# Expert 0's token list summed on chip instead of read back from DRAM

## The chip, the cores and the metric

The kernel runs on one core of a Trainium2 chip. Its engines are named as the profile names them: PE (TensorE), DVE (VectorE), ACT (ScalarE), POOL (GpSimd) and SP (SyncE, which only issues DMAs here). The metric is the device time of one execution in microseconds; the median of three runs is given.

## The reference

Eight heads of memory attention per batch give x, and x goes through a mixture of eight experts in which each row takes the two with the largest noisy logits:

```python
a = softmax(phi, axis=2)                          # 8 batches, 8 heads, 576 rows, 32 memories
k_m, v_m = a^T k, a^T v                           # per batch and head
x = softmax(q k_m^T / 8) v_m                      # 4608 rows of 512
noisy = x @ w_gate + log1p(exp(x @ w_noise)) * noise
top2, top2_w = two largest of 8, softmaxed
for e in range(8):                                # 512 -> 1024 -> 512, all fp32
    out[rows of e] += top2_w * (relu(x[rows of e] @ w1[e]) @ w2[e])
```

## The kernel before, in words

**Attention.** Batches go in four pairs P = 0 to 3. Each batch has two load units (kv, q, phi; u = 0 to 15); each pair has five groups of rows (n = 0 to 19, up to 256 rows each) for which `c_s`, `c_soft1`, `c_soft2`, `c_tr` and `c_av` make scores, softmax, transposition and product. `c_soft2` multiplies by the reciprocal sum on POOL for n < GN and on DVE otherwise. `c_av` also makes the gate logits `lg` and writes the rows to `xs` in DRAM.

**Routing.** `gate(P, j0, j1)` runs once per pair for P = 0, 1, 2 (nine blocks of 128 rows) and in two parts for the last pair. It takes the logits to the two chosen experts (DVE, ending in the mask `gmb`), counts positions within each expert's list with products against a triangle of ones (PE, lines 665 to 670), and turns them to slots: `gidx`, or `pidx` in the last pair (line 692). For P = 0, 1, 2 an entry per row and choice (row id, gate weight) is written by 18 indirect DMAs from POOL into the lists `lst` in DRAM (line 709), from entry tiles `gent0` and `gent1` in turn. `lists` reads them back on SP (line 840) into `ltall` (128 slots x tile x expert).

**Last pair.** Its entries never go through DRAM before they are needed: `onehots` and `onehot_gates` build one-hot matrices of slot and tile on DVE in fp32, PE sums them to 128 x 80 ids and gates, and `merge` adds them into `ltall` after converting the read ids (the CAST of line 590).

**Experts.** Each expert has up to ten tiles of 128 rows. Expert 0's tiles 0 to 5 form the groups g0, g1, g2 of two tiles, which run as early fill for PE among the attention: `gather` fetches the rows with indirect DMAs (line 884), splits them to two f16 halves on ACT and DVE (`ghalf`), and transposes them with a DMA (line 899); `mm1` makes 96 products of 256 columns per group (line 1062), `mm2` 48 of 512 (line 1092). `NEED` says which pair's routing each of g0, g1, g2 needs: (1, 1, 2). Group g3 (tiles 6 to 9, 448 rows) and experts 1 to 7 (products and sums of halves, lines 937 to 1122) follow the last routing. The transposed early rows lie in `stg0`, `stg1`, `stg2`, which expert 1's weight loads also use.

**Order.** A planner gives each step a time from tables of numbers (`PRI`, `ADJ`, `BUF`) and a list scheduler turns the times into one order per engine. `BUF` m0, m1, m2 are the attention groups before which g0, g1, g2 may split their rows.

Of the kernel before, what the change touches and what calls it, by code (L numbers as in the profile page):

```python
# [38 lines left out]
BUF = dict(kvs=3,  phs=3,  qs=2,  et=2,  es=3,  pe=4,  at=3,  xr=4,  st0=1,  st1=1,  ptr=3,  px=2,  mps=3,  xa=3,
           w1=8,  w2=11,  zg=11,  ws=1,  m0=4,  m1=18,  m2=26,  r0=11,  r1=1,  zr=6,  GN=6,  na=1,  nb=22)  # L40
ADJ = dict(s2=(-0.305, -0.749, 0.433, -2.721, 0.107, -0.302, -4.821, -1.222, 0.27, 1.101, 0.051, -0.491, -2.472,
           -2.668, -1.78, -0.576, -2.138, -1.591, -0.804, -1.961),  z=(0.057, -0.272, -1.907, -1.817, -1.721,
           -1.848, -0.055, 0.645, 0, -0.029, -0.085, 1.721, 1.537, 1.865, 1.687, 1.656, 1.687, 2.746, 3.506, 3.003,
           3.003, 1.944, 1.944, 2.087, 1.944, 2.06, 1.944, 1.857, 1.395, 1.512, 1.485, 1.253, 0.1, 1.799, 1.389,
           2.141, 2.115, 3.031),  avb=(0, -1.482, -1.014, -1.627, -1.533, -0.831, -4.141, -3.022, -1.439, -0.672,
           -0.029, -1.474, -2.98, -2.403, -2.514, -2.116, -1.783, -6.14, -2.999, -3.138),  av=(0.104, 0.01, 0.092,
           0.139, 0, 0.031, 0.031, 0.07, -0.107, 0.02, 0, -0.387, -0.146, 0.26, -0.531, 0.259, -0.092, -0.315,
           -0.755, -1.542),  q=(-0.032, 0.356, -0.035, 0.199, -1.248, -1.366, -1.209, -2.207, 0.339, 0.437, -1.488,
           -1.275, -2.053, -2.079, -0.51, -0.981),  x0=(-2.686, -1.628, -7.254),  sc=(0.101, -0.059, -0.105, -0.04,
           -0.678, -0.248, 0.07, 0, 0.024, 0.073, 0.139, -0.272, 0.041, 0.052, -0.001, 0.035, -0.197, -0.204,  # L50
           -0.081, 1.196),  gate=(0.179, 0.04, -0.356, -1.989, -2.923),  tr5=(0.661, -0.092, 0.327, -3.246, -3.536,
           -4.258, -6.146, -7.188, -4.828, -2.528, -0.719, -1.343, -0.369, -0.907, -1.151, -0.76),  y=(1.402, 0.742,
           2.723),  v=(-0.149, -0.589, 1.525, -0.011, -0.077, 0.569, -0.241, -0.303),  kt=(0.854, 0.604, -1.453,
           -0.065, 1.377, 1.758, -0.221, -1.777, -1.698, -1.469, -0.892, -1.509, -1.585, -0.685, -1.829, -2.095),
           kv=(-0.079, 0.034, -0.192, -0.029, 0.829, -0.735, -0.534, -0.477, -0.42, 0.24, 0.66, -0.425, -0.098,
# [1344 lines left out]
```

## Time and profile before

| | us |
|---|---|
| median of 3 runs | 987.38 (985.54 to 989.09) |
| profiled execution | 984.07 |
| its span | 982.1 |

The span runs from the first to the last instruction that the profiler recorded; the execution has 2.0 us more around it. A row of the timeline gives the start, the time it took, the engine and the source line, what was written from what, and in brackets how long the engine had been idle and what released it. In the table of stretches each engine's busy time is followed by its instruction count; PEclk is the granted clock of TensorE as a share of 2.4 GHz.

### The profile page before, as it was taken

The page shows a single profiled execution, that of the slowest core. Times are in us where ns is not written, and L with a number is a line of the kernel's source. Part 1 is how long each engine was busy: PE and PEld are TensorE (multiplying, and loading weights), DVE is VectorE, ACT ScalarE, POOL GpSimd, SP SyncE. Part 2 cuts the span into 40 slices and gives each one's busy share as a digit, 9 for nine tenths or more (in the row PEclk, how much of TensorE's full clock was granted, in tenths as well). Part 3 has the DMA queues.
Part 4 walks back from the last instruction along what each step waited for, and adds up shares of the span by engine and source line. Part 5 has one row for each costly group of instructions (what it writes and reads, how often), then busy time and mean ns, then how long its engine had stood idle before and what let it go on. Part 6 is the DMA issues. An engine that isn't in the chain of part 4 may idle for free.

```text
span 982.1 us, 17769 instructions
## 1 busy us (share of the span) xinstructions
PE 917.5 (93%) x6510; PEld 544.4 (55%) x6510; DVE 626.4 (64%) x1471; ACT 579.8 (59%) x1188; POOL 342.5 (35%) x310
## 2 busy tenths in 40 slices
PE   3898985999899999999999999999999999999994
PEld 2465653677446564646564646464656465656552
DVE  1557788655677585849574957595759575957240
ACT  2586775433547575758665765576567665765240
POOL 3121654724243324535453232323242324240302
PEclk9999987999999999999999999999999999999998
DMA  8999989874878576947795689577947784775403
GB/s 317 323 333 313 362 272 328 239 101 101 153 180 162 110 147 128 212 75 158 132 201 101 140 122 201 91 149 132 208 72 170 137 180 77 169 110 82 63 1 49
DMA packets 197720, 162.03 MB, mean 165 GB/s; under 512 B 151872, under 2 KB 162304, under 8 KB 195584
## 3 DMA queue, kind: packets, MB, share of 16 engines
q1 hardware_dynamic: 177952, 120.43, 50.1%
q0 software_dynamic: 19680, 40.45, 23.5%
q8 instruction: 52, 0.85, 0.4%
q14 instruction: 36, 0.29, 0.1%
HBM read 86.77 MB, written 41.07 MB: 130 GB/s over the span
## 4 chain that ended last, share of the span: by engine, by line
PE 63%; DVE 5%; DMA 5%; issue 3%; ACT 2%; POOL 1%; SPq 0%; POOLq 0%; ACTq 0%
PE ps L1092 19%; PE mp L1092 15%; PE ps L978 14%; PE mp L978 7%; PE pb L978 4%; DMA xt<-ghalf 3%; PE mp L1062 3%; DVE wl L795 1%; DMA gtile<-xs,ltall 1%; DVE wlx L795 1%; POOL out L1122 1%; DVE yw L988 1%; DVE yv L988 1%; DVE gsplit L948 0%; ACT wl L782 0%
## 5 line engine op out<-in xcount | busy, mean ns | idle before, releaser
L1122 POOL DMA_INDIRECT out<-y,ltall x80 | 135.3, 1691 | 258.8 <-ACT y L1104 228.9
L1092 PEld LDWEIGHTS <-hh 128*128 128x128 f16 (+2 forms) x1504 | 122.7, 99 | 144.4 <-issue 17.5
L978 PE MATMUL ps<-xt,wh 128*128 128x320 f16 (+1 forms) x560 | 139.2, 293 | 1.1 <-ACT s L984 0.7
L1092 PE MATMUL ps<-wl,hh 128*128 128x512 f16 (+2 forms) x400 | 125.8, 380 | 0.0
L1092 PE MATMUL ps<-wh,hl 128*128 128x512 f16 (+2 forms) x400 | 125.5, 380 | 0.0
L1092 PE MATMUL ps<-wh,hh 128*128 128x512 f16 (+2 forms) x400 | 122.7, 381 | 0.0
L1092 PE MATMUL mp<-wh,hh 128*128 128x512 f16 (+2 forms) x352 | 113.4, 380 | 0.5 <-DVE hh L1069 0.5
L1092 PE MATMUL mp<-wl,hh 128*128 128x512 f16 (+2 forms) x352 | 113.0, 380 | 0.0
L1092 PE MATMUL mp<-wh,hl 128*128 128x512 f16 (+2 forms) x352 | 112.3, 380 | 0.0
L978 PEld LDWEIGHTS <-wh 128*128 128x128 f16 x896 | 86.6, 98 | 41.5 <-issue 5.8
L1092 PEld LDWEIGHTS <-hl 128*128 128x128 f16 (+2 forms) x752 | 63.2, 99 | 68.9 <-issue 4.9
L978 PE MATMUL ps<-xt,whx 128*128 128x320 f16 (+1 forms) x336 | 96.4, 292 | 0.0
L792 ACT ACTIVATE wh<-stg,wsc 128x512 f16<-128x512 f32 x112 | 76.4, 713 | 31.7 <-DVE wsc L415 20.0
L920 POOL DMA_INDIRECT gtile<-xs,ltall x28 | 34.5, 1233 | 138.8 <-DVE ghalf L948 133.5
L978 PEld LDWEIGHTS <-whx 128*128 128x128 f16 x672 | 65.7, 98 | 27.2 <-issue 2.7
L795 DVE SCALAR_TENSOR_TENSOR wl<-stg,wsc,wh 128x1024 f16<-128x1024 f32 (+1 forms) x63 | 73.1, 1160 | 10.6 <-ACT wh L792 10.2
L978 PE MATMUL ps<-xt,wl 128*128 128x320 f16 (+1 forms) x280 | 72.8, 292 | 0.0
L782 ACT ACTIVATE wl<-stg 128x1024 bf16<-128x1024 f32 x56 | 58.6, 1047 | 23.9 <-DMA stg<-in_w 18.7
L978 PE MATMUL mp<-xt,wh 128*128 128x320 f16 (+1 forms) x224 | 64.9, 293 | 4.1 <-DMA xt<-ghalf 4.1
L709 POOL DMA_INDIRECT lst<-gent,gidx x54 | 54.5, 1009 | 36.2 <-DVE gidx L692 18.5
L920 POOL DMA_INDIRECT gsum<-xs,ltall x42 | 46.3, 1103 | 55.4 <-DVE gsplit L948 44.8
L978 PE MATMUL mp<-xt,whx 128*128 128x320 f16 (+1 forms) x224 | 64.9, 292 | 0.0
(245 smaller groups left out, 1886.8 us busy)
## 6 DMA issues: line engine op xcount, KB each, us to landing
stg<-in_w SPq DMA_DIRECT2D x64, 512.0 KB
kvs<-in_kv SPq DMA_DIRECT2D x16, 1024.0 KB
out<-zt SPq DMA_DIRECT2D x38, 256.0 KB
qs<-in_q_t SPq DMA_DIRECT2D x16, 576.0 KB
xs<-xr SPq DMA_DIRECT2D x36, 256.0 KB
phs<-in_phi_t SPq DMA_DIRECT2D x16, 288.0 KB
kvs<-in_kv SPq DMA_DIRECT2D x16, 128.0 KB
xt<-ghalf SPq DMA_TRANSPOSE x88
```

The source lines that it names most:

```text
L709: sc = G.indirect_dma_start(out=lst[:, :], out_offset=bass.IndirectOffsetOnAxis(ap=idx[:, j, k:k + 1], axis=0), in_=ent[:, j, k, :], in_of ...
L782: (id if first else pace)(A.activation(wl[:, c * 1024:c * 1024 + 1024].bitcast(BF16), s[c], AF.Square, accum_out=am[:, c:c + 1]))
L792: (id if first else pace)(A.activation(h[:, o + k:o + k + 512], x[:, k:k + 512], AF.Identity, scale=sc))
L795: V.scalar_tensor_tensor(l[:, o:o + n], x, sc, h[:, o:o + n], op0=OP.mult, op1=OP.subtract)
L920: G.indirect_dma_start(out=x[:n], out_offset=None, in_=xs[:, :], in_offset=bass.IndirectOffsetOnAxis(ap=ix.bitcast(I32), axis=0))
L978: mark["pe"] = T.matmul(ps[:, :nh], t[w][:, o:o + 128], xt[:, 4 * k0 + 2 * n0 * lo + 2 * (a - k0) + c, :nh], start=(first and m == 0), sto ...
L988: V.scalar_tensor_tensor(y[:, h, :nh], ps[:, :nh], SHC, x[:, :nh], op0=OP.mult, op1=OP.add)
L1062: d = mark["pe"] = mark["mm1", g] = T.matmul(ps[:, :n], ww[:, c * FF + f * 128:c * FF + (f + 1) * 128], xt[:, xo + c, :n], start=(k == 0), ...
L1092: mark["pe"] = T.matmul(ps[lo:lo + x.shape[-1]], x, ws, start=start, stop=stop)
L1122: d = G.indirect_dma_start(out=out[:, :], out_offset=bass.IndirectOffsetOnAxis(ap=LT[e][:n, t, 0:1].bitcast(I32), axis=0), in_=y[:n], in_o ...
```

## The change

For P = 0, 1, 2 the gate now also builds, for expert 0 alone, one-hots of slot (128) and tile (10) and sums ids in two bf16 terms and gates in three. The sums gather in `fsum`; `first_ids` and `first_gates` write expert 0's part of `ltall` from it, so its five list reads go. All 18 scatters per pair stay. `NEED` becomes (0, 1, 2): g0 needs only pair 0's routing. The last pair's one-hots also become bf16 terms. One entry tile serves all pairs. The early rows of g0 and g1 share one load buffer (`scratch`), after the last kv load. GN goes from 6 to 1, and all other numbers of the planner change.

```diff
-           w1=8,  w2=11,  zg=11,  ws=1,  m0=4,  m1=18,  m2=26,  r0=11,  r1=1,  zr=6,  GN=6,  na=1,  nb=22)
+           w1=8,  w2=12,  zg=11,  ws=1,  m0=5,  m1=16,  m2=29,  r0=10,  r1=1,  zr=6,  GN=1,  na=0,  nb=29)
...
-NEED = (1, 1, 2)
+NEED = (0, 1, 2)
...
-    ents = [ac.tile([128, NJ, 2, LW], F32, name="gent%d" % i) for i in range(2)]
...
+    def first_rows(P, ad, ks):
+        pi = gs.tile([128, NJ], I32, name="fpi")
+        pf = gs.tile([128, NJ, 2], F16, name="fpf")
+        cf, m = (gs.tile([128, NJ], F32, name=x) for x in ("fcf", "fm"))
+        pos = ad[:, :, 0]
+        V.tensor_copy(pi, pos)
+        V.tensor_tensor(m, ks[0][:, :, 0], ks[1][:, :, 0], OP.add)
+        V.tensor_scalar(pi, pi, 127, None, op0=OP.bitwise_and)
+        V.tensor_copy(pf, pi[:, :, None].to_broadcast([128, NJ, 2]))
+        V.tensor_tensor(cf, pos, pi, OP.subtract)
+        V.tensor_scalar(cf, cf, 1.0 / 128, 1.0, op0=OP.mult, op1=OP.add)
+        V.tensor_tensor(cf, cf, m, OP.mult)
+        row = gs.tile([128, NJ, 5, NTL + 1], BF16, name="fterms")
+        one = gs.tile([128, NJ, NTL + 1], F32, name="fone")
+        wide = [128, NJ, NTL + 1]
+        V.tensor_tensor(one, ftab[:, None, 128:].to_broadcast(wide), cf[:, :, None].to_broadcast(wide), OP.is_equal)
+        V.scalar_tensor_tensor(row[:, :, 0], fid[:, :, None].to_broadcast(wide), float(P * TP), one, op0=OP.add, op1=OP.mult)
+        V.tensor_scalar(row[:, :, 1], one, fpart, None, op0=OP.mult)
+        return pf, row, one
+
+    def first_sums(P, ks, ent, pf, row, one):
+        g, h = (gs.tile([128, NJ], F32, name=x) for x in ("fcf", "fm"))
+        V.tensor_tensor(g, ks[0][:, :, 0], ent[:, :, 0, 1], OP.mult)
+        V.tensor_tensor(h, ks[1][:, :, 0], ent[:, :, 1, 1], OP.mult)
+        V.tensor_tensor(g, g, h, OP.add)
+        V.tensor_tensor(one, one, g[:, :, None].to_broadcast([128, NJ, NTL + 1]), OP.mult)
+        for i in range(2, 5):
+            V.tensor_copy(row[:, :, i], one)
+            if i < 4:
+                V.tensor_tensor(one, one, row[:, :, i], OP.subtract)
+        ps = ptr.tile([128, 512], F32, name="tr")[:, 0:5 * (NTL + 1)]
+        for j0, n in ((0, 5), (5, 4)):
+            oh = sm.tile([128, 4, 128], F32, name="at", bufs=BUF["at"]).rearrange("p a q -> p (a q)").bitcast(BF16)
+            oh = oh[:, 0:n * 128].rearrange("p (a q) -> p a q", a=n)
+            V.tensor_tensor(oh.rearrange("p a (q r) -> p a q r", r=2),
...
+                            pf[:, j0:j0 + n, None, :].to_broadcast([128, n, 64, 2]), OP.is_equal)
+            for j in range(n):
+                T.matmul(ps, oh[:, j], row[:, j0 + j].rearrange("p c t -> p (c t)"), start=(j0 + j == 0), stop=(j0 + j == NJ - 1))
+        V.tensor_tensor(fsum.rearrange("p c t -> p (c t)"), fsum.rearrange("p c t -> p (c t)"), ps, OP.add)
+        for g in range(3):
+            if NEED[g] == P:
+                first_ids(slice(2 * g, 2 * g + 2))
+                first_gates(slice(2 * g, 2 * g + 2))
+
+    def first_ids(t):
+        n = t.stop - t.start
+        f = gs.tile([128, 2, NTL + 1], F32, name="fo")
+        o, i = f[:, 0, 0:n], f[:, 1, 0:n]
+        V.tensor_tensor(i, fsum[:, 0, t], fsum[:, 1, t], OP.add)
+        V.scalar_tensor_tensor(o, i, 0.0, fnone[:, t], op0=OP.is_equal, op1=OP.mult)
+        V.tensor_tensor(ltall[:, 0, t, 0].bitcast(I32), o, i, OP.add)
+
+    def first_gates(t):
+        x = ltall[:, 0, t, 1]
+        V.tensor_tensor(x, fsum[:, 2, t], fsum[:, 3, t], OP.add)
+        V.tensor_tensor(x, x, fsum[:, 4, t], OP.add)
...
-            T.matmul(pg[:, 0:NS], oh[:, a, :], rid[:, a, :], start=(a == 0), stop=(a == n - 1))
+            T.matmul(pg[:, 0:2 * NS], oh[:, a, :], ids[:, a].rearrange("p c q -> p (c q)"), start=(a == 0), stop=(a == n - 1))
...
-            T.matmul(pg[:, NS:2 * NS], oh[:, a, :], oc[:, a, :], start=(a == 0), stop=(a == n - 1))
+            T.matmul(pg[:, 2 * NS:5 * NS], oh[:, a, :], gates[:, a].rearrange("p c q -> p (c q)"), start=(a == 0), stop=(a == n - 1))
...
+        if not last:
+            mine = first_rows(P, ad, ks)
...
-            ent = ents[len(ents_used) % 2]
-            ents_used.append(0)
+            ent = pent
...
+        if not last:
+            first_sums(P, ks, ent, *mine)
...
-            last = NEED[t0 // 2] if e == 0 and t0 < 6 else NP - 2
+            last = NP - 2
...
-            late["x0", g] = mpool.tile([128, 1024], F32, name="stg%d" % g)
+            if g == 0:
+                late["x0"] = scratch()[:, 0:2048].rearrange("p (g x) -> p g x", g=2)
+            late["x0", g] = late["x0"][:, g] if g < 2 else mpool.tile([128, 1024], F32, name="stg%d" % g)
...
-        t = end = add(t + max(0.0, adj("x0", g)), lists, e, ts[0], ts[-1] + 1)
+        t = end = max(t + max(0.0, adj("x0", g)), kv_at[0] + 0.01 if g < 2 else t)
...
-            add(t, lists, 0, 6, NTL + 1)
```

**The order on POOL, from pair 1's scatters to pair 2's.** `lst<-gent` and `lst<-pent` are scatters, `gtile<-xs` gathers of expert 0's early rows, `vb` attention's. Before:

```order
L375 TENSOR_TENSOR vb_1858<-vm_1848,vmask_105 128x256
L709 DMA lst_58<-gent1_121,gidx_1972 38016x16 x15
L375 TENSOR_TENSOR vb_2070<-vm_2060,vmask_105 128x256
L709 DMA lst_58<-gent1_121,gidx_1972 38016x16 x3
L375 TENSOR_TENSOR vb_2180<-vm_2170,vmask_105 128x256
L884 DMA gtile_2339<-xs_57,ltall_124 128x512
L884 DMA gtile_2341<-xs_57,ltall_124 128x512
L884 DMA gtile_2426<-xs_57,ltall_124 128x512
L709 DMA lst_58<-gent0_120,gidx_2511 38016x16 x15
L884 DMA gtile_2428<-xs_57,ltall_124 128x512
L709 DMA lst_58<-gent0_120,gidx_2511 38016x16 x3
```

After, from pair 0's scatters:

```order
L812 DMA lst_58<-pent_125,gidx_1387 38016x16 x18
L991 DMA gtile_2113<-xs_57,ltall_127 128x512
L991 DMA gtile_2115<-xs_57,ltall_127 128x512
L388 TENSOR_TENSOR vb_1514<-vm_1504,vmask_105 128x256
L388 TENSOR_TENSOR vb_1626<-vm_1616,vmask_105 128x256
L786 IOTA pent_125 128x18
L388 TENSOR_TENSOR vb_1825<-vm_1815,vmask_105 128x256
L388 TENSOR_TENSOR vb_1937<-vm_1927,vmask_105 128x256
```

The two gathers of g0 stood behind pair 1's scatters and now stand right behind pair 0's; nothing lies any more among the scatters of a pair.

**The order on ACT, where g0's rows are split.** `xr` are copies of finished attention rows (`c_av`), `es` of transposed weights (`a_tr1`, `a_tr5`), `ghalf` the split, `gex` and `gu` the gate's. Before:

```order
L697 ACTIVATE gex_2521<-gex_2521 128x9
L499 ACTIVATE at_2551<-tr_2546 128x512
L499 ACTIVATE at_2594<-tr_2591 128x256
L895 ACTIVATE ghalf_2359<-gtile_2339 128x512
L515 ACTIVATE xr_2615<-xp_2616,sv_2281 128x272
L895 ACTIVATE ghalf_2363<-gtile_2341 128x512
L515 ACTIVATE xr_2615<-xp_2619,sv_2281 128x272
L499 ACTIVATE at_2685<-tr_2680 128x512
```

After:

```order
L340 ACTIVATE et_1856,ssum_1857<-phs_1852,nmx_1854 128x576
L413 ACTIVATE vb_1626<-tr_1725 128x16
L528 ACTIVATE xr_1774<-xp_1775,sv_1164 128x272
L528 ACTIVATE xr_1774<-xp_1778,sv_1164 128x272
L1002 ACTIVATE ghalf_2155<-gtile_2113 128x512
L349 ACTIVATE es_1761<-tr_1762 128x512
L373 ACTIVATE es_1761<-tr_1771 64x128
L528 ACTIVATE xr_1774<-xp_1782,sv_1164 128x272
L1002 ACTIVATE ghalf_2159<-gtile_2115 128x512
L528 ACTIVATE xr_1774<-xp_1785,sv_1164 128x272
L365 ACTIVATE kk_1813<-tr_1792,rs_1587 128x128
```

Before, the split stood behind `gex` of pair 2's gate; now it stands ahead of `gu` of pair 1's, between copies of one attention group.

**The order on DVE, where the read lists are converted for the last part.** `kvs<-ltall` is the conversion, `lg` and `gu`, `gm`, `gi`, `gk` the last part's gate, `hh` and `hl` mm1's outputs, `gmb` the mask that PE waits for. Before:

```order
L590 CAST kvs_2780<-ltall_124 128x4
L590 CAST kvs_2780<-ltall_124 128x70
L1069 CAST hh_2661<-r_3235 128x256
L1070 TENSOR_TENSOR hl_2662<-r_3235,hh_2661 128x256
L520 TENSOR_TENSOR lg_2560<-xr_2860 128x32
L630 TENSOR_TENSOR lg_2560<-lg_2560,isb_2278 128x64
L1069 CAST hh_2661<-r_3252 128x256
L1070 TENSOR_TENSOR hl_2662<-r_3252,hh_2661 128x256
L632 TENSOR_SCALAR gr_2908<-gu_2906 128x32
```

After:

```order
L759 TENSOR_TENSOR gmb_3166<-gk0_3154,gk1_3164 128x32
L802 TENSOR_TENSOR pent_125<-isb_2369,gden_3225 128x4
L803 TENSOR_TENSOR pent_125<-gex_3224,gden_3225 128x4
L690 CAST kvs_3010<-ltall_127 128x70
L776 TENSOR_TENSOR gk_3177<-gk_3177,tr_3168 128x32
L777 TENSOR_TENSOR base_62<-base_62,tr_3168 128x8
L791 TENSOR_TENSOR gu_3183<-gk_3177,gk0_3154 128x32
L791 TENSOR_TENSOR gln_3186<-gk_3177,gk1_3164 128x32
L236 TENSOR_TENSOR olim_3312<-olim_3312,base_62 128x216
L792 TENSOR_REDUCE gai_3182<-gu_3183 128x4
```

The conversion stood ahead of the last part's whole gate and now stands behind its mask, ahead only of the step from positions to slots.

## Rows read from the trace of the kernel before

**Rows 1.** The page, part 1: busy us, share of the span, instructions.
```profile
PE 917.5 (93%) x6510; PEld 544.4 (55%) x6510; DVE 626.4 (64%) x1471; ACT 579.8 (59%) x1188; POOL 342.5 (35%) x310
```

**Rows 2.** Stretches: length, busy PE, PEld, DVE, ACT, POOL; granted clock; DMA.
```profile
0.00:77.80 77.80, 58.07 (x622) 36.29 (x622) 31.68 (x117) 47.34 (x142) 18.04 (x52) 0.98 0.96 328
...
92.97:130.88 37.91, 35.65 (x427) 23.12 (x426) 30.15 (x126) 31.49 (x93) 22.47 (x27) 1.00 0.92 313
130.88:170.80 39.92, 26.41 (x190) 16.67 (x190) 36.50 (x133) 23.74 (x59) 23.04 (x23) 0.76 0.94 318
170.80:257.40 86.60, 79.71 (x562) 56.21 (x561) 48.65 (x180) 31.33 (x73) 36.50 (x34) 0.99 0.72 155
257.40:982.10 724.70, 706.25 (x4581) 405.49 (x4581) 466.70 (x854) 438.36 (x803) 241.77 (x173) 0.99 0.69 130
```

**Rows 3.** Waits, 77 to 260 us: total us, times, longest us.
```profile
PE tr L665 <- DVE gmb L659: 7.9, 2, 7.7
...
ACT ghalf L895 <- DMA gtile<-xs,ltall: 17.2, 4, 9.2
```

**Rows 4.** Timeline of GpSimd, one row of ScalarE: start, us, then the instruction.
```profile
93.27 1.19 POOL L709 DMA_INDIRECT lst<-gent,gidx  x1 [12.21 <-DVE gidx L692]
...
116.11 1.19 POOL L709 DMA_INDIRECT lst<-gent,gidx  x1 [0.30 <-issue]
...
195.03 0.96 POOL L709 DMA_INDIRECT lst<-gent,gidx  x1 [0.30 <-issue]
...
201.10 1.45 POOL L884 DMA_INDIRECT gtile<-xs,ltall  x1 [5.11 <-DMA ltall<-lst]
...
205.63 0.63 ACT L895 ACTIVATE ghalf<-gtile 128x512 f16<-128x512 f32 x1 [9.23 <-DMA gtile<-xs,ltall]
...
236.70 1.02 POOL L884 DMA_INDIRECT gtile<-xs,ltall  x1 [2.01 <-DVE ltall L592]
...
243.08 1.05 POOL L884 DMA_INDIRECT gtile<-xs,ltall  x1 [0.30 <-DVE ghalf L898]
```

**Rows 5.** Timeline of the DMA queue of SyncE.
```profile
198.43 12.89 SPq L840 DMA_DIRECT2D ltall<-lst  x17
211.42 2.63 SPq L899 DMA_TRANSPOSE stg<-ghalf  x2
```

**Rows 6.** Timeline of VectorE.
```profile
170.62 0.18 DVE L692 CAST gidx<-gai 128x18 int32<-128x18 f32 x1
...
213.37 0.20 DVE L590 CAST kvs<-ltall 128x70 f32<-128x70 int32 x1 [0.99 <-DMA ltall<-lst]
...
227.74 0.16 DVE L692 CAST pidx<-gai 128x8 int32<-128x8 f32 x1
...
236.26 0.35 DVE L592 TENSOR_TENSOR ltall<-kvs 128x4 int32<-128x4 f32 x2
```

**Rows 7.** Instructions of VectorE by line and form: total us, mean ns.
```profile
L701 DVE TENSOR_TENSOR gent<-isb,gden 128x9 f32<-128x9 f32 x3 | 0.5, 168 | 0.0
...
L653 DVE TENSOR_TENSOR gk<-iota_e,gi 128x72 f32<-128x72 f32 x6 | 1.4, 241 | 0.1
...
L470 DVE TENSOR_TENSOR pe<-tr,mx 128x512 f32<-128x512 f32 x1 | 0.7, 692 | 0.0
...
L557 DVE TENSOR_TENSOR kvs<-kvs 128x640 f32<-128x640 f32 x1 | 0.8, 825 | 0.0
```

**Rows 8.** TensorE: timeline, then one group of instructions (170 to 260 us).
```profile
169.19 0.38 PE L670 MATMUL tr<-gmb,ones_bf 128*128 128x8 bf16 x9
...
179.76 1.04 PE L1062 MATMUL mp<-stg,wh 128*128 128x256 f16 x8
...
191.00 0.38 PE L1092 MATMUL mp<-wh,hh 128*128 128x512 f16 x1
...
191.22 0.38 PE L1092 MATMUL mp<-wh,hl 128*128 128x512 f16 x1
...
L562 PE MATMUL tr<-kvs 128*128 128x80 f32 x36 | 4.4, 276 | 0.0
```

More of the change, by code (lines that the diff above doesn't have):

```diff
@@ new lines, in onehots, with part @@
+        V.tensor_tensor(pc, ai.rearrange("p k j -> p j k"), pi, OP.subtract)
+        V.tensor_scalar(cf, pc[:, :, :, None].to_broadcast([128, nj, 2, 2]), 1.0 / 128, None, op0=OP.mult)
+        def part(x, o, c, q):
+            return x[:, o:o + n * c * q // 2].bitcast(BF16).rearrange("p (a c q) -> p a c q", a=n, c=c)
+        ids, gates = part(big, 0, 2, NS), part(big, n * NS, 3, NS)
+        oc = part(*((big, n * 200) if j0 else (late["oc"], 0)), 1, NS)[:, :, 0]
+        oh = part(*((big, n * 240) if j0 else (late["oh"], 0)), 1, 128)[:, :, 0]
@@ new lines, in two, with tab, per @@
+        def two(x):
+            return x.rearrange("p a (q r) -> p a q r", r=2)
+        def tab(x):
+            return x.rearrange("p (q r) -> p q r", r=2)[:, None].to_broadcast([128, n, x.shape[-1] // 2, 2])
+        def per(x, w):
+            return x.rearrange("p j k r -> p (j k) r")[:, :, None, :].to_broadcast([128, n, w // 2, 2])
+        V.tensor_tensor(two(oc), tab(late["tiles"]), per(cf, NS), OP.is_equal)
+        V.tensor_scalar(ids[:, :, 1], oc, late["pv"], None, op0=OP.mult)
+        for j in range(nj):
+            V.tensor_tensor(two(ids[:, 2 * j:2 * j + 2, 0]), two(oc[:, 2 * j:2 * j + 2]),
+                            late["hi"][:, j0 + j, None, None, :].to_broadcast([128, 2, NS // 2, 2]), OP.mult)
@@ L568, in onehot_gates @@
+        return oh, oc, pg, gates, two, per, gt
+    def onehot_gates(j0, nj, ent, oh, oc, pg, gates, two, per, gt):
         n = 2 * nj
[L569 to L570 removed]
+        g = gt[:, 0:n].rearrange("p (j k) -> p j k", k=2)
+        V.tensor_copy(g, ent[:, :, :, 1])
+        for i in range(3):
+            h = gt[:, (i + 1) * n:(i + 2) * n].bitcast(BF16).rearrange("p (j k r) -> p j k r", k=2, r=2)
+            V.tensor_copy(h, g[:, :, :, None].to_broadcast([128, nj, 2, 2]))
+            if i < 2:
+                V.tensor_tensor(g, g, h[:, :, :, 0], OP.subtract)
+            V.tensor_tensor(two(gates[:, :, i]), two(oc), per(h, NS), OP.mult)
@@ L832, in prep @@
         yield
+    for e in range(E):
+        LT[e], LX[e] = ltall[:, e], lxall[:, e]
     def lists(e, t0, t1):
-        LT[e], LX[e] = ltall[:, e], lxall[:, e]
         lt = LT[e]
```

174 lines of the change are left out of this document (93 added, 81 removed).

## Prediction

> **What bounds the kernel now.** I read the busy shares first: TensorE works 917.5 of 982.1 us [rows 1]. A table of stretches then says where the rest lies [rows 2]. From 257.40, where the first product on group 3's rows starts, TensorE is busy 706.25 of 724.70 us; the change leaves that work as it is. Before 257.40 it is busy 211.3 us and idle 46. So the change can only move the point at which the last stretch begins. Two things hold that point up.
>
> The first is VectorE between the routing of pair 0 and that of pair 2. From 130.88 to 170.80 it works 36.50 of 39.92 us while TensorE works 26.41, at a granted clock of 0.76 (part of the stretch at the lower of its two levels, 1.2 and 2.4 GHz, in a stretch in which it often waited). TensorE's longest wait here is 7.7 us for gmb, VectorE's mask of the routed experts [rows 3].
>
> The second is a chain from pair 2's routing on: gidx, the slots, at 170.62 [rows 6], the 18 scatters until 195.99 [rows 4], the 17 list reads from 198.43 to 211.32 [rows 5], the conversion of the read lists at 213.37, the last part's routing right behind it, its slots (pidx) at 227.74, the merged lists at 236.26 [rows 6], and group 3's gathers and transposes until 257.40. TensorE has other work beside it (79.71 of 86.60 us in [rows 2]).
>
> **The change part by part.** *Lists on chip, VectorE.* A pair gets 27 more instructions: 16 of 2 to 50 columns at about 0.17 us, nine of 90 columns at about 0.26 (0.24 is measured at 72), and one-hots of 640 and 512 columns, which cost 0.83 and 0.69 by the rows of that width with fp32 sources [rows 7]. That is 2.7 + 2.3 + 1.5 = 6.5 us per pair. Between gidx of pairs 0 and 2 stand most of pair 0's, all of pair 1's and the first of pair 2's, about 13 us, and group 0's two subtractions (2 x 0.69), which before came later: 14.5 us.
>
> The nearest rows for the one-hots read fp32; the new ones read and write 16-bit elements, which no row of two sources here does. The Trainium skill, "VectorE: DVE Perf Modes", "The perf-mode tier table", gives a two-source operation on 16-bit data in SBUF twice the fp32 rate. By that the two one-hots would cost about 0.8 us rather than 1.5, an estimate; three pairs and the last part's one-hots would make the sum some 3 us shorter.
>
> *TensorE.* Nine products 50 columns wide and nine weight loads per pair: L670's nine, 8 wide, take 0.38 us and the wide ones 0.22 each [rows 8], so 0.4 to 2 us; I take 1.5, so 3 before pair 2's slots. Group 0's 48 second products of 512 columns follow each other by 0.22 us (191.00, 191.22), its 96 first ones of 256 columns by half, 0.11 (eight take 1.04 with the last one's tail): 10.5 each, 21 us [rows 8]. They stood after pair 2's routing and now stand before it. In the last pair 18 fp32 products for ids, which the trace splits into 36, take 4.4 us, and there are as many for gates; as bf16 of 160 and 240 columns they take at most 36 x 0.11: 4.5 us saved, most of it beside other work.
>
> *ScalarE and VectorE waiting.* Group 0's two copies to f16 now stand in ScalarE's order between two units' work, before the routing of pair 1. Their gathers stand behind pair 0's 18 scatters on GpSimd. Eighteen took 24.0 us, one other instruction of about 0.9 among them [rows 4], so 23.1 apart from it; a gather issued at 201.10 was copied at 205.63 [rows 4], 4.5 later. Everything behind these copies on ScalarE waits if it gets there early; such a copy already waited 9.2 us [rows 3]. TensorE likewise stands at pair 0's products until VectorE has done some 33 instructions after gmb, about 7 us at the prices above, with one product of attention as cover.
>
> *Smaller edits.* One entry tile instead of two: the next pair's entries wait for 23 us of scatters, while gidx of two pairs lie 38 us or more apart, so nothing, or the difference if the gates close up. Five of GpSimd's softmax products go to VectorE, 5 x 0.69 = 3.5 us, hidden while VectorE works 31.68 of 77.80 us [rows 2]. Group 0's and 1's rows in a load buffer let expert 1's weights load sooner: nothing, since what bounds the last stretch is TensorE itself. Expert 0's five list reads go (17 at 0.76 in [rows 5]; 14 now stand behind pair 2's scatters).
>
> **The sum.** *Pair 0's slots.* 92.97 before. About 7 us more of TensorE's work stands ahead of this gate, partly in holes of its first 77 us, and some 3 us of the new instructions on VectorE: 97 (94 to 100).
>
> *From there to pair 2's slots*, 77.8 us before. VectorE alone needs 66.65 + 14.5 = 81, TensorE 62.06 + 21 + 3 less some 3 for the clock = 83, and neither ran without waits: VectorE's own were 11 us. If the fill keeps both supplied, 81; with the old waits and the new ones of ScalarE and TensorE on top, 97. I take 88, nearer to the lower end because both had much less queued ahead of them in the old 39.92 us. That puts gidx of pair 2 at 185 (175 to 197), 14 later than before.
>
> *From there to group 3.* Scatters without an interruption 23.1; 2.4 to the first read (195.99 to 198.43); 14 reads at 0.76 and two transposes between them at 1.3 (2.63 for two in [rows 5]), 13.2; 2.1 until the conversion: 40.8, where it was 42.8. The conversion now stands behind the last part's gmb, and only its slots behind it, 1.5 us: pidx comes 42.3 after gidx of pair 2, where it was 57.1. From pidx to merged lists there were 8.5 us; VectorE's splitting into terms adds some 2: 10.5. From lists to 257.40 there were 21.1; the fourth gather of group 3 is issued right behind the third, no longer behind two gathers of expert 1 (243.08, 6.4 after the first; back to back 3.9), 2.5 sooner, of which I count 1.8, since its split also waits for buffers: 19.3. Together 72.1 instead of 86.6. TensorE has 79.7 - 21 - 4.5 + 1.5 = 56 us to do in this, so it isn't what ends it.
>
> Group 3 then starts at 185 + 72.1 = 257.1, as before. The last 11 second products of group 2 (11 x 0.22 = 2.4), which ran among group 3's, are done by then. The span is 982.1 - 0.3 - 2.4 = 979.4, the execution 2.0 more (984.07 for 982.1), and the median of the runs shown lies 3.3 above the profiled execution: **985 us**. Gain and cost cancel when gidx of pair 2 comes at 187.7; each us of it is one of the result.
>
> **The rivals.** *The queues stay full (977).* VectorE's extra work replaces its waits, and gidx of pair 2 comes near 177, 80 us behind pair 0's 97, with no wait left on VectorE. For it: 13.5 us of holes on TensorE in one stretch, at 0.76 of the clock, just where 21 us of independent products now stand. Against it: TensorE's waits were on VectorE, and that gets 14.5 us more. 985 - 8 = 977.
>
> *Group 0's gathers block ScalarE (994).* At 97 the gathers go out at 120.4 and the copy can run at 125. ScalarE reaches it some 6 to 9 us earlier, holds up the transposition copies and VectorE's subtractions queued in front of pair 1's gate, and so both gates behind it. Nothing of it comes back, since VectorE is full until pair 2: gidx at 194, 987.4 + 6.3 = 994. It decides from a stall of about 3 us beyond the 88. For it: the measured 9.2 us of the same wait. Against it: ScalarE has its share of two more attention groups ahead of the copies in its order, and it is itself held by VectorE's longer list.
>
> *The change doesn't do what it says (988).* The lists of expert 0 no longer wait for reads, but the 14 others still do, and the conversion still holds the last part: if the last part's logits are late too, from units 14 and 15, pidx comes 45 or more after gidx of pair 2 and the shorter chain is lost.
>
> **How the numbers follow.** Forecast case, 985 (gidx of pair 2 at 182 to 190, so 982 to 990): 0.39. Full queues: 0.28. Blocked ScalarE: 0.28. No shorter chain: 0.05. The range leaves a tenth at each end of these: from gidx at 174 to 196, 974 to 997. A measurement of this kernel tells 0.3%, about 3 us, from no change. Faster by that: all of the full queues and 0.14 of the forecast case, 0.42. Within it: 0.23 of the forecast case, 0.02 of each of the last two, 0.27. Slower: 0.26 + 0.03 + 0.02 = 0.31.
>
> **What would show it.** Right: gidx of pair 2 near 185 with VectorE over 90% busy from pair 0's slots on; pidx of the last part some 42 us after it; the conversion waiting for list reads; group 3's first product near 257, TensorE idle 10 us or more in front of it. Wrong: gidx of pair 2 before 178 or behind 195; ScalarE's wait for group 0's gather over 9 us; pidx 50 us after gidx; a wait of TensorE for expert 1's weights.

## The result and the profile after

The kernel after takes 996.75 us (994.98 to 997.70, 4 runs), the kernel before on the same chip 986.46 us (984.37 to 989.09, 4 runs): a ratio of 1.0101, with a 95% interval of 1.0071 to 1.0131. The change costs about 10 us. The forecast was 985 with a range of 974 to 997, so the time lies at the range's upper end and on the other side of no change. The profiled execution after took 997.70 us, the slowest of its four, its span 995.7; the one before was a quick one, 984.07, so the two profiles lie 13.6 us apart where the medians lie 10.3.

The page after, part 1, answers to [rows 1]: TensorE does 3.6 us more, VectorE 10 us more.

```profile
PE 921.1 (93%) x6503; PEld 542.5 (54%) x6503; DVE 636.3 (64%) x1594; ACT 580.5 (58%) x1188; POOL 343.4 (34%) x312
```

The table of stretches of the kernel after answers to [rows 2]: length, busy time of PE, PEld, DVE, ACT and POOL, granted clock, DMA. The borders are `gidx` of pairs 0, 1 and 2 (96.27, 159.48, 195.48) and the first product on group 3's rows (270.79).

```profile
96.27:159.48 63.21, 51.06 (x533) 32.24 (x534) 44.24 (x174) 37.20 (x105) 24.90 (x31) 0.84 0.73 237
159.48:195.48 36.00, 34.61 (x236) 22.27 (x233) 32.37 (x146) 23.29 (x52) 20.57 (x21) 1.00 0.82 281
195.48:270.79 75.31, 55.51 (x373) 36.88 (x373) 42.94 (x212) 22.97 (x53) 37.74 (x36) 0.91 0.69 147
270.79:995.70 724.91, 706.73 (x4573) 405.24 (x4573) 466.26 (x853) 437.60 (x802) 244.69 (x172) 0.99 0.70 129
```

The last stretch is as long as before, 724.91 against 724.70 us. All of the loss is that it begins 13.4 us later, at 270.79 instead of 257.40. Pair 0's slots come 3.3 us later, as forecast; the rest arises in one row. From pair 0's slots to pair 1's it takes 63.21 us where it took 37.91 [rows 2], and both engines that were meant to be kept busy stand in it: VectorE works 44.24 of it, TensorE 51.06. The next row gives only 3.9 back (36.00 for 39.92), and the chain from pair 2's slots to group 3 gives 11.3 (75.31 for 86.60), as the change intends.

Where the time went in the long row is told by the waits of the two engines. First TensorE's waits up to 280 us of the kernel after (total us, times, longest us), which answer to [rows 3]:

```profile
PE tr L576 <- DVE fterms L565: 7.8, 2, 7.3
PE mp L1169 <- DMA xt<-ghalf: 7.5, 1, 7.5
...
PE tr L362 <- ACT es L349: 4.9, 2, 4.4
PE mp L1169 <- DMA stg<-ghalf: 2.9, 1, 2.9
```

Then the places, in its timeline, with one row of VectorE, one of GpSimd and one of ScalarE:

```profile
96.26 0.82 DVE L572 TENSOR_TENSOR at<-ftab,fpf 128x640 bf16<-128x640 f16 x2
...
101.81 0.54 PE L576 MATMUL tr<-fterms,at 128*128 128x50 bf16 x9 [7.29 <-DVE fterms L565]
102.17 0.67 PE L510 MATMUL tr<-identf,pe 128*128 128x128 f32 x2
...
119.97 1.00 POOL L991 DMA_INDIRECT gtile<-xs,ltall  x1 [0.30 <-DVE ss L501]
...
125.37 0.63 ACT L1002 ACTIVATE ghalf<-gtile 128x512 f16<-128x512 f32 x1 [4.11 <-DMA gtile<-xs,ltall]
...
126.53 2.52 PE L362 MATMUL tr<-kvs,es 128*32 128x128 f32 x40 [4.38 <-ACT es L349]
```

Two instructions sit at the head of an engine's order before their inputs are there. TensorE reaches the nine products that sum pair 0's lists and stands 7.29 us until VectorE has the terms. ScalarE reaches the split of group 0's first gathered rows and stands 4.11 us; the copy `es` behind it comes late, and TensorE stands 4.38 us for that. What stands behind them in the order waits as well: the products right behind the nine (L510) have their source from VectorE by 98.04 at the latest and run at 102.17.

In pair 1's routing the order on the two engines shows a second time. VectorE has the mask at 139.03; TensorE counts on it at 156.49, 17.5 us later, and of the 17.23 us between it works 15.59, 6.0 of them on group 0's first products. For nearly all of that time it had other work first. The slots come at 159.31.

```profile
139.03 0.23 DVE L759 TENSOR_TENSOR gmb<-gk,gk 128x72 bf16<-128x72 f32 x1
...
156.49 0.20 PE L765 MATMUL tr<-gmb,tri 128*128 128x72 bf16 x1
...
159.31 0.17 DVE L793 CAST gidx<-gai 128x18 int32<-128x18 f32 x1
...
195.31 0.17 DVE L793 CAST gidx<-gai 128x18 int32<-128x18 f32 x1
```

The chain from pair 2's slots on answers to [rows 4 to 6]. GpSimd's 18 scatters run from 196.26 to 219.97. SyncE reads the lists from 221.19; VectorE's conversion of what was read has waited 10.30 us when it starts (the profile names the DMA issued right behind the reads, `lst<-onone` at 237.75, as the one that came last), and behind it come the last part's slots (`pidx`), its one-hots, and the ids with which group 3's gathers can go.

```profile
221.19 9.90 SPq L945 DMA_DIRECT2D ltall<-lst  x8
...
241.68 0.20 DVE L690 CAST kvs<-ltall 128x70 f32<-128x70 int32 x1 [10.30 <-DMA lst<-onone]
...
242.99 0.16 DVE L793 CAST pidx<-gai 128x8 int32<-128x8 f32 x1
...
251.06 0.16 DVE L589 TENSOR_TENSOR ltall<-fo 128x4 int32<-128x4 f32 x1
...
270.79 1.65 PE L1169 MATMUL mp<-xt,wh 128*128 128x448 f16 x4 [7.47 <-DMA xt<-ghalf]
```

So three theories went to the chip. **Sums**: pair 0's sums stand too early on TensorE. **Group 0**: its place, right behind pair 0's routing, makes pair 1's and pair 2's slots late. **Conversion**: it stands ahead of the last part's slots and of group 3's ids, which since the change need no list read. The rival to all three is that the planner's new numbers give a worse order as such.

### The profile page after: what moved, and what is told of

Same layout as the page of the kernel before. It is cut to its first block, busy times and chain, and to the rows that moved or that the text cites. A ratio compares the mean times of both kernels' runs of the same rounds, so it can differ in the third digit from the quotient of the medians.

```text
span 995.7 us, 17859 instructions
## 1 busy us (share of the span) xinstructions
PE 921.1 (93%) x6503; PEld 542.5 (54%) x6503; DVE 636.3 (64%) x1594; ACT 580.5 (58%) x1188; POOL 343.4 (34%) x312
## 4 chain that ended last, share of the span: by engine, by line
PE 70%; DVE 11%; DMA 7%; issue 4%; ACT 4%; POOL 2%; SPq 1%; POOLq 0%; ACTq 0%
PE ps L1199 19%; PE mp L1199 15%; PE ps L1085 14%; PE mp L1085 7%; PE pb L1085 4%; DMA xt<-ghalf 3%; PE tr L362 2%; PE xp L526 2%; PE xp L402 2%; PE mp L1169 2%; DMA gtile<-xs,ltall 1%; DVE wl L898 1%; POOL lst L812 1%; DMA phs<-in_phi_t 1%; DVE wlx L898 1%
## 5 line engine op out<-in xcount | busy, mean ns | idle before, releaser
L1027 POOL DMA_INDIRECT gsum<-xs,ltall x42 | 50.0, 1192 | 57.1 <-DVE gsplit L1055 46.8
L812 POOL DMA_INDIRECT lst<-pent,gidx x54 | 54.8, 1014 | 35.4 <-issue 14.3
```

The lines of the kernel that those rows point to most:

```text
L812: sc = G.indirect_dma_start(out=lst[:, :], out_offset=bass.IndirectOffsetOnAxis(ap=idx[:, j, k:k + 1], axis=0), in_=ent[:, j, k, :], in_of ...
L1027: G.indirect_dma_start(out=x[:n], out_offset=None, in_=xs[:, :], in_offset=bass.IndirectOffsetOnAxis(ap=ix.bitcast(I32), axis=0))
```

## The experiments

The runs fell on several chips, and of two kinds. On some of them, called the first kind here, the kernel before takes 985 to 986 us, on four others, the second kind, 1036 to 1039 (the last section tells what those show). A ratio is always to runs of the kernel before on the same chip; chips of the two kinds are not compared with each other. Each edit makes the planner lay the order anew, so a part of each difference can be due to small moves elsewhere; that is why the gates are read beside the times.

### The order as such

The first run puts the planner's old numbers (`PRI`, `BUF`, `ADJ`) into the kernel after, and leaves all else.

> The changed code, with its early group 0, under the tables of numbers of the kernel before (order, buffers, which engine multiplies). If the new order is what costs: 985 to 991. If the code costs by its sums and by the early group 0, whatever the order: 993 or more.

Measured on a chip of the second kind: 1061.13 us against 1036.18, a ratio of 1.0233 (1.0185 to 1.0281). The unedited kernel after has 1.0041 (1.0015 to 1.0067) on another such chip:

> The changed kernel unedited, on the chip of the other runs of this call, for the comparison and for its trace there. If the chip is like the first: 1.010 of the kernel before. If its attention stage is stalled from outside (waits that the trace gives to no engine), the ratio may be anything from 0.99 to 1.02, and the edits are read against this run.

The old order is worse for the changed code, not better, at least on chips of the second kind. So the loss isn't made by leaving the old numbers; whether other numbers would suit the changed code better was not tried.

### The sums behind the slots

```diff
-        if not last:
-            first_sums(P, ks, ent, *mine)
         yield
         if last:
             onehot_gates(j0, nj, ent, *mine)
             return
+        first_sums(P, ks, ent, *mine)
```

The sums are issued one step of the gate later, in the code right ahead of the scatters.

> The changed kernel with the sums of pairs 0 to 2 issued one step of the gate later, so that TensorE has some 60 instructions of attention between a gate's counting and the sums. In the changed kernel TensorE stood 7.3 us before pair 0's sums. If that stall is lost for good: pair 1's and 2's slots come 5 to 7 us sooner and the kernel takes 990 to 992. If VectorE or what follows takes it up: under 2 us, 995 to 997; if group 0's gathers now come later and hold ScalarE longer, 997 to 1000.

> The changed kernel with the sums one step later alone. With the group 0 edit on top it gave 1.0068 where slots of pair 2 came 6.6 us sooner and the conversion's wait took 4.5 us of that back. Theory (the stall at the sums is the loss, pair 1's place is not): 1.004 to 1.009. Rival (pair 1's place in TensorE's order is the loss): 1.009 to 1.012.

On a chip of the second kind: 1028.13 against 1036.18, 0.9932 (0.9903 to 0.9961). On one of the first kind: 991.02 us against 985.45, 1.0047 (1.0007 to 1.0086), instead of 1.0101. Its profile, taken of the quickest of its four executions (987.74 us), shows the products without a wait, the slots of pairs 1 and 2 at 152.60 and 189.14, 6.7 and 6.2 us earlier than after, and group 3 at 261.64, 9 us earlier:

```profile
120.40 0.40 PE L576 MATMUL tr<-fterms,at 128*128 128x50 bf16 x9
...
130.47 0.63 ACT L1001 ACTIVATE ghalf<-gtile 128x512 f16<-128x512 f32 x1 [4.47 <-DMA gtile<-xs,ltall]
...
149.04 0.21 PE L765 MATMUL tr<-gmb,tri 128*128 128x72 bf16 x1
...
152.60 0.17 DVE L793 CAST gidx<-gai 128x18 int32<-128x18 f32 x1
...
189.14 0.17 DVE L793 CAST gidx<-gai 128x18 int32<-128x18 f32 x1
...
261.64 0.92 PE L1168 MATMUL mp<-xt,wh 128*128 128x448 f16 x4 [0.46 <-DMA xt<-ghalf]
```

The wait of ScalarE is still there (4.47), and so is the late count of pair 1. The two further kernels with this edit and group 0's place of after have slots of pair 2 at 188.69 and 189.07. The first theory holds and is worth 6 to 7 us at pair 2's slots. Of the time it is some 5 us by the medians on chips of the first kind, where its interval still touches after's; on those of the second kind it is some 11 us by the ratios, more than expected, and the two intervals lie apart (on two chips).

### Group 0's products behind pair 1's count

```diff
         for k in range(nj):
-            T.matmul(pc, ones_bf, mbf[:, k * E:(k + 1) * E], start=(k == 0), stop=(k == nj - 1))
+            mark["gate", P] = T.matmul(pc, ones_bf, mbf[:, k * E:(k + 1) * E], start=(k == 0), stop=(k == nj - 1))
...
+                if e == g == k == 0:
+                    after(d, "gate", 1)
```

This keeps group 0 on pair 0's routing, and moves only TensorE's work on it behind pair 1's counting products. It was run alone and with the later sums.

> The changed kernel with one edit: group 0's first products may not start on TensorE before pair 1's counting. That puts pair 1's counting some 70 rows earlier in TensorE's order; before, its mask waited 17.5 us for its turn. If that wait is what makes pair 2's routing late: pair 1's slots 10 us or more sooner and the kernel 5 to 10 us faster than the changed one. If the products only fill time in which TensorE would stand for other engines, then pair 2's slots don't move: within 3 us of the changed kernel, or slower.

> Two edits: the sums of a pair one step later, group 0's first products behind pair 1's counting; the conversion stays where the changed kernel has it. If the conversion's wait for list reads is hidden where the attention stage is long (the edit of it alone moved nothing): within 3 us of the kernel with all three, 0.986 to 0.991 of the kernel before. If it counts once the rest is shorter: 3 to 8 us above it.

Alone: 1.0032 (1.0006 to 1.0059) on a chip of the second kind, where the kernel after has 1.0041. The times don't tell the two apart, but the slots of pairs 1 and 2 come 5.6 and 3.5 us earlier there. First the kernel with the edit, then the kernel after on that chip:

```profile
172.81 0.17 DVE L793 CAST gidx<-gai 128x18 int32<-128x18 f32 x1
...
230.55 0.17 DVE L793 CAST gidx<-gai 128x18 int32<-128x18 f32 x1
```

```profile
178.40 0.17 DVE L793 CAST gidx<-gai 128x18 int32<-128x18 f32 x1
...
234.07 0.17 DVE L793 CAST gidx<-gai 128x18 int32<-128x18 f32 x1
```

With the later sums, on a chip of the first kind: 991.55 against 985.41, 1.0068 (1.0045 to 1.0091), where the later sums alone have 1.0047 on another. The count moves from 149.04 to 145.03, the slots do not:

```profile
145.03 0.20 PE L765 MATMUL tr<-gmb,tri 128*128 128x72 bf16 x1
...
153.09 0.17 DVE L793 CAST gidx<-gai 128x18 int32<-128x18 f32 x1
...
236.12 0.20 DVE L690 CAST kvs<-ltall 128x70 f32<-128x70 int32 x1 [11.87 <-DMA lst<-onone]
...
268.71 1.65 PE L1168 MATMUL mp<-xt,wh 128*128 128x448 f16 x4 [11.17 <-DMA xt<-ghalf]
```

So once the sums are later, TensorE's work on group 0 ahead of pair 1's count is not what holds up the slots: with the count 4 us earlier, they come no earlier. With the early sums it has a share in the slots, as the run alone shows. And moving it has a price behind the slots: group 3 starts at 268.71, 7.1 us later than with the later sums alone, after a wait of 11.17 us of TensorE for its rows.

### Group 0 on pair 1's routing again

```diff
-NEED = (0, 1, 2)
+NEED = (1, 1, 2)
```

> The changed kernel with group 0 on the routing of pair 1, as before the change, and nothing else undone (same tables, sums on chip). In the changed kernel the mask of pair 1 was ready at 139.03 and TensorE took it at 156.49, behind half of group 0's first products and other work. If early group 0 is what delays pair 1's and 2's routing: slots of pair 1 some 15 us and of pair 2 some 10 us sooner, 985 to 990. If the time is lost to the sums on chip themselves: 994 to 998.

> The sums one step later and group 0 on the routing of pair 1, as before the change. If the early group 0 is a loss by itself: at or under the kernel with the sums later alone, 0.985 to 0.993 of the kernel before. If it pays once the stall at the sums is gone, because it fills TensorE between pair 0 and pair 2: 5 to 10 us slower than that, 0.998 to 1.003.

Alone, on a chip of the second kind, the expectation was missed: 1049.61 against 1036.18, 1.0134 (1.0076 to 1.0192), where the kernel after on another such chip has 1.0041. It had no run on a chip of the first kind, so what it does alone stays open; in its profile pair 1's slots come at 159.32 and pair 2's at 239.78, 19.1 us sooner and 5.7 later than in the kernel after on such a chip. Together with the later sums, on a chip of the first kind: 985.23 us against 985.41, 0.9988 (0.9962 to 1.0014), where the kernel with the later sums, group 0 early and its products moved has 1.0068 (1.0045 to 1.0091) on the same chip. By its number this lies in the range of the reading that early group 0 pays, but that range was set from the later sums' 0.9932 on a chip of the second kind; on the first kind they have 1.0047 (on another chip, the intervals touch), and the early group is the slower one. The gates:

```profile
125.82 0.20 PE L765 MATMUL tr<-gmb,tri 128*128 128x72 bf16 x1
...
129.05 0.17 DVE L793 CAST gidx<-gai 128x18 int32<-128x18 f32 x1
...
183.08 0.17 DVE L793 CAST gidx<-gai 128x18 int32<-128x18 f32 x1
...
255.79 0.92 PE L1168 MATMUL mp<-xt,wh 128*128 128x448 f16 x4
```

Pair 1's slots come 23.6 us earlier than with the later sums alone, pair 2's 6.1, group 3 5.9. ScalarE's wait for a gathered row falls from 4.47 to 0.90 us. The theory on group 0 holds as far as its place goes, once the sums are later. Which part of the early group costs was not separated: the gathers ahead of attention's copies on ScalarE, its splits on VectorE, or its products on TensorE. With the edit of the section above and the later sums, these products stand behind pair 1's count, but still ahead of pair 2's slots: TensorE spends 25 us on them between the slots of pairs 0 and 2 there, 24 in the kernel after, and 7 in this one.

### The conversion behind the ids

```diff
-        first_ids(slice(6, NTL + 1))
+        ids = first_ids(slice(6, NTL + 1))
         x = ltall[:, 1:, :, 0].bitcast(I32)
-        V.tensor_copy(o[:, 1:], x)
+        cast = V.tensor_copy(o[:, 1:], x)
+        tc.add_manual_dep(cast.ins, ids.ins.name, SYNC, reason="expert 0 first")
```

`first_ids` returns its last instruction here.

> The changed kernel with one edit: the conversion of the read lists (experts 1 to 7) on VectorE may only run after expert 0's last ids, which need no read. In the changed kernel VectorE stood 10.3 us before that conversion with the last part's slots queued behind it. If that wait sets the start of group 3: slots and group 3 come some 8 us sooner, bounded by TensorE's 12 us of waits in front of group 3, so 986 to 990. If the start of group 3 is set by something else (TensorE's own queue), no more than 2 us: 994 to 997.

> The changed kernel with the conversion of the read lists behind expert 0's last ids, on an undisturbed chip if this is one. Theory: VectorE's 10.3 us before the conversion hold the last part's slots and with them group 3: group 3 some 8 us sooner, 0.998 to 1.003 of the kernel before. Rival: TensorE's own queue sets group 3's start (it waits 7.5 us right before it, so at least that much is free): under 2 us, 1.008 to 1.012.

On a chip of the second kind: 1.0063 (1.0037 to 1.0088), no gain over the 1.0041 of after; the conversion waited only 4.38 us in the profile of after on such a chip. On one of the first kind: 991.71 against 985.45, 1.0060 (1.0023 to 1.0097). That lies between its two cases, and the interval overlaps after's, so the time alone doesn't settle it. The timeline of VectorE says how little came through:

```profile
234.43 0.16 DVE L794 CAST pidx<-gai 128x8 int32<-128x8 f32 x1
...
241.77 0.29 DVE L1177 CAST hh<-r 128x256 f16<-128x256 f32 x1 [5.84 <-ACT r L1176]
241.98 0.48 DVE L645 TENSOR_TENSOR kvs<-kvs,gcf 128x640 bf16<-128x640 f16 x1
...
248.72 0.16 DVE L589 TENSOR_TENSOR ltall<-fo 128x4 int32<-128x4 f32 x1
...
249.37 0.20 DVE L690 CAST kvs<-ltall 128x70 f32<-128x70 int32 x1
```

`pidx` comes 8.6 us earlier (234.43 for 242.99), the ids only 2.3 (248.72 for 251.06), group 3 2.6 (268.18). Between them VectorE now stands 5.84 us at the conversion of group 2's first outputs, `hh`, which wait for group 2's transposed rows; the last part's one-hots are queued behind. One instruction at the head of the queue has taken the place of another.

The same edit on top of both earlier ones, and without the one on TensorE:

> All three edits. If each loss is separate: 18 to 24 us under the changed kernel, which would be 1 to 1.5% under the kernel before. If pair 1's place in the order is of no account: as with the two edits, within 3 us.

> All three edits. Without the conversion's edit VectorE waited 11.9 us before it and TensorE 9.7 and 11.2 us for group 2's and group 3's rows. Theory (the conversion is the last wait on the chain): group 3 some 9 to 11 us sooner than in that kernel, 0.994 to 0.998 of the kernel before. Rival (rows of group 2 or TensorE's work end last): 1.002 to 1.007.

> The changed kernel with two edits: the sums of a pair issued one step later, and the conversion of the read lists behind expert 0's last ids. If the stall of 7.3 us at the sums and the wait of 10.3 us at the conversion are separate losses on one chain, the gains add: 12 to 16 us under the changed kernel. If the first makes the second vanish or TensorE's own work takes its place: 6 to 9 us under it.

All three: 986.06 against 985.45 on a chip of the first kind, 1.0005 (0.9963 to 1.0047), level with before and between its two cases; group 3 starts at 261.78 where the same kernel without the later conversion, on another chip of that kind, had 268.71. The sums alone had 261.64, so there the conversion only takes back what the edit on TensorE had cost. On one of the second kind: 0.9883 (0.9853 to 0.9912), 16.5 us under after. Sums and conversion without the edit on TensorE: 0.9934 (0.9906 to 0.9962) on that chip, 10.5 us under after, no better than the sums alone on another (0.9932). Both gains lie between the cases expected. The edit on TensorE is worth 6 us beside the other two there (1024.64 us against 1030.69), though pair 2's slots come 2.2 later with it (223.71 for 221.50); group 3 comes 4.7 earlier, and why was not found. So on chips of the first kind the conversion is worth 2.6 us at group 3's start by itself, 6.9 with the other two, and (below) 4.6 beside group 0's old place; the traces show it, the times alone hardly do: the two kernels with and without it have 1.0005 (0.9963 to 1.0047) and 1.0068 (1.0045 to 1.0091).

### All that helped together

The later sums, the later conversion, and group 0 on pair 1's routing:

> The sums later, group 0 on pair 1's routing again, and the conversion behind expert 0's last ids. Without the last edit it was 0.9988, with TensorE not waiting in front of group 3 and the conversion waiting 5.5 us. Theory (TensorE's own work ends last there): within 2 us of that, 0.997 to 1.001. Rival (the conversion's wait still counts): 0.992 to 0.996.

> The version that came out best (sums later, group 0 on pair 1's routing, conversion behind expert 0's last ids), against the kernel before, with more executions: its first interval was 0.9925 to 1.0019. If the conversion's wait still counted in it, 0.992 to 0.996; if TensorE's own work ends last, 0.997 to 1.001.

982.55 us against 985.45 on a chip of the first kind: 0.9972 (0.9925 to 1.0019). 1025.12 against 1036.13 on one of the second: 0.9891 (0.9875 to 0.9908), below both cases expected. By these ratios it is 1.3 to 1.5% quicker than after on either kind of chip. Against before it is clearly quicker only on the second kind; on the first the interval includes no change. Its rows of VectorE and TensorE, on the first kind and from the quickest of its four executions (979.20 us):

```profile
217.16 0.16 DVE L794 CAST pidx<-gai 128x8 int32<-128x8 f32 x1
...
226.62 0.16 DVE L589 TENSOR_TENSOR ltall<-fo 128x4 int32<-128x4 f32 x1
...
227.55 0.20 DVE L690 CAST kvs<-ltall 128x70 f32<-128x70 int32 x1 [0.77 <-DMA lst<-onone]
...
251.21 0.92 PE L1169 MATMUL mp<-xt,wh 128*128 128x448 f16 x4 [0.23 <-ACT r L1175]
```

The conversion waits 0.77 us, where without its edit it waited 5.48. Group 3 starts 6.2 us earlier than before (257.40) and 19.6 earlier than after. Its span is 977.4, so the last stretch takes 726.19 us, 1.5 more than before: a little of the gain is given back there.

## Why the prediction was wrong

**What failed: the 88 us from pair 0's slots to pair 2's.** They took 99.2 (96.27 to 195.48), 11.2 more, and that is most of the 16.3 us by which the span was missed: 979.4 us of predicted span, less 0.7 for pair 0's slots (96.3 for 97), plus 11.2, plus 3.2 for the rest of the chain (75.3 for 72.1), plus 2.6 for the last stretch, give the 995.7 measured. The work itself was counted about right. VectorE did 44.24 + 32.37 = 76.6 us of it where 81 were expected, TensorE 51.06 + 34.61 = 85.7 where 83 were (group 0's products took 24.3 of it, for 21). The waits were not: VectorE stood 22.6 us and TensorE 13.5.

The text had both new waits and their prices. It gave TensorE "about 7 us" at pair 0's products (7.29 measured) and put the sum with all waits at 97. It then took 88, "because both had much less queued ahead of them in the old 39.92 us". That step is wrong, and a run shows it for TensorE's wait: without it pair 2's slots come 6.2 us sooner. In these rows TensorE starts its instructions in their order (L510 stands until 102.17 behind the nine, with its source there at 98.04); work queued behind the one that waits doesn't fill its wait. Only what stands ahead of it does, and that was named too: "one product of attention". The sum should have been made with the waits in it, 97 or more, which gives 994. The 97 is small for its own terms, too: 81 of work, VectorE's old 11 and TensorE's 7 make 99, with nothing yet for ScalarE. That this comes so near the 99.2 is in part luck, as VectorE worked less than the 81 and stood longer.

**The clock.** TensorE was to win 3 us back by running at the higher level. It didn't: the granted clock is 0.84 in the 63.21 us with the two waits, 10.1 us' worth of full speed not granted, where 0.76 in 39.92 us before [rows 2] is 9.6. (Part of either lies in waits, where it costs nothing.) With the later sums, which end the longer of the two waits, it is 0.94 in that row.

**The rival "Group 0's gathers block ScalarE".** It had pair 2's slots at 194 (195.3 came) and 994 us. Its times were good: the gathers at 120.4 (119.97) and the copy at 125 (125.37). But ScalarE came there 4.1 us early, not 6 to 9, and half of what the two edits give at pair 2's slots (6.2 of 12.2 us) was TensorE's stand at the sums, which the later sums remove while this wait stays. So the rival came nearest with at most half of the cause. Later sums and group 0's old place together bring pair 2's slots to 183.1. That the sums and that place made them late is shown by runs; the share of ScalarE's wait is argued, since with group 0 some 17 us of its products moved behind these slots, too.

**Full queues (977).** Refuted by the same waits. Of the signs that were to show the forecast right, VectorE over 90% busy from pair 0's slots on didn't come (77% up to pair 2's); of those that were to show it wrong, pair 2's slots behind 195 came (195.3). **No shorter chain (988).** Its sign came and its result didn't: `pidx` stands 47.7 us after `gidx` of pair 2, past the 45 at which the text saw the shorter chain lost, though not for late logits but for the conversion's wait. Still the chain is 11.3 us shorter than before.

**The chain to group 3, 72.1 forecast and 75.3 measured.** Scatters 24.5 (23.1), first read 1.2 after them (2.4), reads and transposes 16.5 (13.2), conversion 4.0 later (2.1), `pidx` 1.5 (1.5), lists 8.1 (10.5), group 3's rows 19.6 (19.3). The reads were mis-sized, by 3.3 us: the first eight took 9.90 us, 1.24 each, where [rows 5] has 0.76. That the conversion would wait for the reads was foreseen, and so were the holes of TensorE in front of group 3 ("10 us or more"; 2.89, 7.47 and 1.96 at the one-hots' products). What was not seen is that the wait is needless, since expert 0's ids no longer come from the reads. That the 19.3 held is luck: the fourth gather of group 3, which was to follow the third at once, came 6.4 us after the first (251.50 and 257.89), as late as before.

**Bounds that held.** The nine products took 0.54 and 0.39 us, at the lower end of 0.4 to 2. The single entry tile, counted as nothing, made VectorE wait 2.88 us at the entries of the first part of the last pair (211.37), beside the 10 us that it then waited for the reads.

The one-hots with 16-bit elements cost 0.48 and 0.42 us at 640 and 512 columns, and 0.68 at 1024, where the rows with fp32 have 0.83 and 0.69 [rows 7] and 1.21. First the three forms after, then the widest one before (total us, mean ns):

```profile
L572 DVE TENSOR_TENSOR at<-ftab,fpf 128x640 bf16<-128x640 f16 x3 | 1.4, 483 | 0.0
L572 DVE TENSOR_TENSOR at<-ftab,fpf 128x512 bf16<-128x512 f16 x3 | 1.2, 415 | 0.0
...
L650 DVE TENSOR_TENSOR kvs<-kvs,gpf 128x1024 bf16<-128x1024 f16 x1 | 0.7, 680 | 0.0
```

```profile
L559 DVE TENSOR_TENSOR kvs<-kvs,gpf 128x1024 f32<-128x1024 f32 x1 | 1.2, 1211 | 0.0
```

By the Trainium skill, "VectorE: DVE Perf Modes", "The perf-mode tier table", a two-source operation on 16-bit data in SBUF runs at twice the fp32 rate; the trace nearly agrees, with 1.71 times at 640 columns, 1.67 at 512 and 1.78 at 1024. It made the forecast's work a little too large, and could not turn its sign.

**The last 2.4 us** for second products of group 2 were not found: the last stretch is no shorter. Among the kernels here on chips of the first kind it is between 720.5 and 726.8 us long with the same work in it; what sets that stays open.

## What to carry to other kernels

When instructions are moved so that they fill an engine's holes, look at what stands at the head of its order at that time: a filler helps only if it stands ahead of the instruction that waits. Put a small dependent product, a copy behind a gather or a conversion of what a DMA reads as late as its users allow, and after each such move look for the next instruction that waits there. When a forecast has a price for each new wait, leave those waits in the sum unless a row shows what is queued ahead of them.

## What the runs showed of the hardware

On four of the chips the kernels here took 1025 to 1061 us. Before and after were hit alike: 1036.18 and 1041.18 us, 50 and 44 more than on the chip of the result. The granted clock of the span is lower there as well (0.95 for 0.98). Engines stand there for long while GpSimd's 18 scatters of a pair run, and up to 6 us past their end. First two rows of the timeline of the kernel after on such a chip; then three of the kernel before, one in each pair's scatters:

```profile
125.58 0.37 ACT L365 ACTIVATE kk<-tr,rs 128x128 f32<-128x128 f32 x1 [21.95 <-remote]
...
262.15 0.29 DVE L1176 CAST hh<-r 128x256 f16<-128x256 f32 x1 [16.74 <-issue]
```

```profile
119.27 0.37 ACT L352 ACTIVATE kk<-tr,rs 128x128 f32<-128x128 f32 x1 [17.28 <-remote]
...
177.90 0.37 ACT L352 ACTIVATE kk<-tr,rs 128x128 f32<-128x128 f32 x1 [18.49 <-remote]
...
232.41 0.38 ACT L1068 ACTIVATE r<-mp 128x256 f32<-128x256 f32 x1 [13.67 <-remote]
```

These waits of 14 to 22 us have no releaser in the profile other than "remote" or "issue", and SyncE's queue issues nothing for 31.7 us around the first of them. In the profiles from the other chips the longest such wait between pair 0's slots and 300 us is one of 9.3 us, of GpSimd in the kernel before. The last stretch is no longer there (719.6 us after, 726.2 before). The run of the kernel before that gave these rows:

> The kernel before, unedited, for its trace beside those of the edits. If the chip holds up both kernels alike during the scatters of a pair (waits of ScalarE or VectorE of 10 to 20 us that no engine ends), the slots of pair 2 come at about 205 to 215 instead of 170.6 and the kernel takes 1036; if only the changed kernel is held up there, the slots of pair 2 come at 171 to 175.

It took 1038.83 us beside 1037.61, with pair 2's slots at 208.46, so both kernels are held up alike. What holds the engines was not found; no run here changes the scatters.
